# Attention and a two-layer MLP in one pass: the first score blocks and the due times of batches 1 to 3

## The chip, the cores and the metric

The kernel runs on one core of a Trainium2 chip. The metric is device time in microseconds (us) of one execution. Before the change three runs took 661.99, 661.43 and 659.28 us; their median is 661.43 us.

## The reference

Causal attention over 4 batches, 12 heads, 448 positions and 64 dimensions, all in fp32, feeds an MLP whose middle is h · clip(h + 3, 0, 6) / 6:

```python
scores = scale * np.matmul(q, k.transpose(0, 1, 3, 2))
scores = np.where(np.triu(ones, k=1), -1e9, scores)
attn = np.exp(scores - max(scores)); attn = attn / (sum(attn) + 1e-09)
x = np.matmul(attn, v)            # to 1792 tokens x 768
h = x @ w_in                      # 768 x 2048
g = h * np.clip(h + 3.0, 0.0, 6.0) / 6.0
return (g @ w_out).astype(np.float32)   # 2048 x 768
```

## The kernel before

**Tiles.** The 448 positions are cut in four blocks of 112 (C). Two heads make a pair; there are six pairs (NPAIR) of each batch. The first block of all four batches at once is done by `first_pair` (six times, pairs 0 to 5), since it only attends to itself: scores 112x112 for each batch and head, with the four batches side by side in a tile of 112x448. The other three blocks of a batch are done by `pair`, 24 times. The MLP runs in five groups: group 0 on the 448 tokens of the first blocks, groups 1 to 4 on the 336 other tokens of batches 0 to 3. A group is 96 steps: 16 blocks of 128 rows of `w_in` (three steps each) and six of 128 outputs of `w_out` (eight steps each).

**Precision.** Each fp32 factor is split into a high part and a remainder (`xh`, `xl` of the input, `wh`, `wl` of a weight, `gh`, `gl` of the gate), and `triple` makes three matmuls of each product: lines 598 to 600. In group 0 the weights come as pairs of 32-bit words of int64 and the values are put together by three bit operations on VectorE for each chunk of 384 or 512 columns (`bits`, lines 571, 573 and 576) before the cast to `wh` (ScalarE) and the subtraction for `wl` (GpSimd or VectorE); the result is also kept in DRAM for the groups behind. A block of `w_in` has two chunks, so six bit operations.

**first_pair before.** On TensorE: the mask is added by a matmul (line 322), then 16 instructions of products q·k (329). On VectorE: row maximum of either head (336). The two heads then go different ways. Head 1: the maximum is scaled (342), and ScalarE makes four exponentials of 112x112 (348), each with its own bias and a sum given out by an extra accumulator read. Head 0: VectorE subtracts the maximum (356), ScalarE makes one exponential of 112x448 (360), VectorE sums (363). Then for both heads the inverse of the sums (369, 370), the scaling on GpSimd (377), a transpose on TensorE into bank `mo` (386), a copy to `pt` on ScalarE or VectorE (238 or 241), the product with v (399), and `x_split` into `xh` and `xl`. A matmul of group 0 reads the `x` of all six pairs, so group 0 starts when pair 5 is through.

**What sets the order.** The class `Flow` plans everything ahead: each operation has a key (a due time in steps), the engines that may do it with an assumed duration, and the buffers it needs; at each moment an engine of the plan takes the ready operation of lowest key. What the planner decides is then written out as a fixed order of each engine; on the chip every engine works through its own list in order. The assumed durations thus set the order and nothing else. All DMAs are issued by SyncE (SP), in the planned order. Keys of the first loads are near -900; `T_FIRST`, `T_EARLY` and `T_REST` are the due times of the first blocks, of the pairs of batch 0 (every 13 steps), and of the pairs of batches 1 to 3 (every 16 steps).

PSUM has eight banks: six `s` (scores, bit operations, transposes and products with v of `pair`) and two `mo` (accumulators of the MLP, transposes of `first_pair`). There are three buffers each of `wh`, `wl` and `op` (weight words put together, and operands of `pair`) and four of `wd` (raw weight words).

Of the kernel before, what the change touches and what calls it, by code (L numbers as in the profile page):

```python
# [50 lines left out]
T_FIRST, T_EARLY, T_REST, T_LOAD, T_W, T_WLOAD = -66, 4, -16, -24, 9, 9  # L51
# [139 lines left out]
def tile_causal_attention_hardswish_moe(ctx: ExitStack, tc: tile.TileContext, q, k, v, w_in, w_out, out):  # L191
# [66 lines left out]
    three = const.tile([128, 1], F32, tag="three", name="three")  # L258

    def setup():  # L260
# [12 lines left out]
        nc.vector.tensor_copy(maskr, mask[:, R:].unsqueeze(1).to_broadcast([C, B, C]))  # L273
# [20 lines left out]
    def by_batch(x):  # L294
        return x.rearrange("m (b s) -> m b s", b=B)

    def first_pair(p):
        t = T_FIRST + 8 * p
        for a, src in enumerate((q, k)):
            dma(  # L300
                -900 + 4 * p, 230e3, lambda a=a: by_batch(ap(first_qk)[:, 2 * p + a]),
                lambda src=src: src[:, p, :, :, :C].rearrange("b e d s -> (e d) b s"),
                w=[(first_qk, p, a)],
            )
# [29 lines left out]
        for e in (1, 0):  # L334
            one(
                t + 1, {"D": 1}, elem(S), lambda _, e=e: nc.vector.tensor_reduce(row(e, 0), sc[e](), AX.X, ALU.max),
                [(ps[e], 0)], [(st, e, 0)],
            )
            if e:
                one(  # L340
                    t + 1, {"D": 1}, .25,
                    lambda _: nc.vector.tensor_scalar(row(1, 0), row(1, 0), -0.125, None, ALU.mult),
                    [], [(st, 1, 0)],
                )
        for b in range(B):
            one(
                t + 2, {"A": 1}, .6,
                lambda _, b=b: nc.scalar.activation(
                    pb[1]()[:, b], sc[1]()[:, b], ACTF.Exp, bias=ap(st)[:, 1, b:b + 1], scale=0.125,
                    accum_out=ap(st)[:, 1, 4 + b:5 + b],  # L350
                ),
                [(ps[1], 0), (st, 1, 0)], [(pr[1], b), (st, 1, 4 + b)],
            )
        allb = [(pr[0], b) for b in range(B)]
        one(
            t + 2, {"D": 1}, elem(S), lambda _: nc.vector.tensor_tensor(pb[0](), sc[0](), wide(0, 0), ALU.subtract),
            [(ps[0], 0), (st, 0, 0)], allb,
        )
        one(
            t + 2, {"A": 1}, .65, lambda _: nc.scalar.activation(pb[0](), pb[0](), ACTF.Exp, scale=0.125), [], allb,  # L360
        )
        one(
            t + 3, {"D": 1}, elem(S), lambda _: nc.vector.tensor_reduce(row(0, 4), pb[0](), AX.X, ALU.add),
            allb, [(st, 0, 4)],
        )
# [6 lines left out]
        sums = [(st, 0, 4)] + [(st, 1, 4 + b) for b in range(B)]  # L372
        one(t + 3.5, {"D": 1}, .5, inverse, [], sums + [("sums", p)])
        for e in (1, 0):
# [5 lines left out]
                sums, [(pr[e], b) for b in range(B)],  # L380
# [7 lines left out]
            pe(t + 10 - e, [(.4, turn, [(tp, 0)])], [(pr[e], b) for b in range(B)])  # L388
# [213 lines left out]
    def group(g):  # L602
# [107 lines left out]
```

## Time and profile before

| what | value |
|---|---|
| median of three runs | 661.43 us (659.28 to 661.99) |
| the profiled execution | 661.54 us |
| its span, first to last instruction | 659.8 us |
| TensorE busy | 643.9 us, 98% |
| VectorE / ScalarE / GpSimd busy | 71% / 56% / 46% |
| mean granted TensorE clock | 0.992 of 2.4 GHz |

The profiled execution is 1.7 us longer than its span, which is the time around the first and the last instruction. A busy TensorE is not a TensorE at its peak: matmuls overlap, and a matmul counts as busy from its start to its modelled end. Where the spacing of matmuls matters, the starts of rows are compared. A line of the timeline has the start, the duration from that start to the end of the last of its instructions, the engine, the line of code, the tiles, a count and, in brackets, the idle time before it and what ended that.

### The profile page before, as it was taken

To read this page: it belongs to the slowest core of one execution; us is meant where nothing else is said; L and a number is where in the kernel's file an instruction comes from. 1 tells how busy PE (TensorE), PEld (TensorE's weight loads), DVE (VectorE), ACT (ScalarE), POOL (GpSimd) and SP (SyncE) were. 2 spreads that over 40 slices of the span, in tenths; PEclk is the share of its full clock that TensorE was granted. 3 is DMA by queue.
4 is the path that set the end of the run, shared out by engine and by line. 5 is a ranking of instruction groups with operands and counts; after the bars stand their busy time and mean duration, and the time that the engine had idled before them with its cause. 6 is when DMAs were issued, how large, how long until landed. Compare 5 with 4: busy or idle time off the path is not lost.

```text
span 659.8 us, 12245 instructions
## 1 busy us (share of the span) xinstructions
PE 643.9 (98%) x4236; PEld 587.3 (89%) x4236; DVE 465.8 (71%) x939; ACT 367.3 (56%) x870; POOL 301.2 (46%) x333
## 2 busy tenths in 40 slices
PE   7689999999999999999999999999999999999998
PEld 5569887878889999999999999999999999999997
DVE  4889898977687798854588795567798743566432
ACT  3665656654546666555576664656666554444342
POOL 1667667546572686423375563433676410011100
PEclk9979999999999999999999999999999999999999
DMA  9989876888788543556744547555553334643452
GB/s 232 259 267 298 265 242 192 260 282 295 206 265 246 158 144 107 159 171 182 217 152 135 154 127 206 157 168 186 161 168 87 112 113 132 209 139 110 139 164 65
DMA packets 66878, 120.89 MB, mean 183 GB/s; under 512 B 16896, under 2 KB 33408, under 8 KB 66816
## 3 DMA queue, kind: packets, MB, share of 16 engines
q1 hardware_dynamic: 66816, 120.11, 60.7%
q8 instruction: 33, 0.54, 0.3%
q14 instruction: 29, 0.24, 0.1%
HBM read 101.99 MB, written 18.09 MB: 182 GB/s over the span
## 4 chain that ended last, share of the span: by engine, by line
PE 92%; DVE 3%; DMA 1%; SPq 1%; ACT 1%; POOL 1%; issue 1%; DVEq 0%; ACTq 0%; POOLq 0%
PE mo L598 24%; PE mo L600 23%; PE mo L599 23%; PE s L535 6%; PE s L516 6%; PE s L450 3%; PE s L451 2%; PE s L453 2%; DMA gh<-in_k_dram 1%; SPq L229 1%; PE s L399 1%; DVE s L571 1%; DVE s L573 1%; DVE op L576 0%; PE s L329 0%
## 5 line engine op out<-in xcount | busy, mean ns | idle before, releaser
L250 DVE TENSOR_TENSOR wl<-wd,wh 128x512 fp32r<-128x512 f32 (+1 forms) x159 | 142.8, 898 | 99.8 <-ACT wh L238 99.5
L238 ACT CAST wh<-wd 128x512 fp32r<-128x512 f32 (+1 forms) x160 | 112.9, 706 | 120.0 <-PE mo L599 85.9
L598 PE MATMUL mo<-xh,wh 128*128 128x336 f32 (+1 forms) x480 | 160.8, 335 | 0.1
L598 PE MATMUL mo<-gh,wh 128*128 128x336 f32 (+1 forms) x480 | 159.2, 332 | 0.0
L600 PE MATMUL mo<-xh,wl 128*128 128x336 f32 (+1 forms) x480 | 157.2, 327 | 0.0
L600 PE MATMUL mo<-gh,wl 128*128 128x336 f32 (+1 forms) x480 | 156.9, 327 | 0.3 <-POOL wl L250 0.3
L599 PE MATMUL mo<-gl,wh 128*128 128x336 f32 (+1 forms) x480 | 156.4, 326 | 0.0
L599 PE MATMUL mo<-xl,wh 128*128 128x336 f32 (+1 forms) x480 | 156.2, 325 | 0.0
L505 POOL TENSOR_SCALAR pr<-pr,prow 112x224 f32<-112x224 f32 x144 | 109.0, 773 | 39.5 <-DVE prow L493 39.3
L476 DVE CUSTOM_DVE_ANT_0 s<-s,mask 112x448 f32<-112x448 f32 (+1 forms) x144 | 70.6, 527 | 39.7 <-PE s L451 33.1
L245 POOL TENSOR_SCALAR gh<-r 128x336 fp32r<-128x336 f32 x51 | 33.3, 654 | 138.2 <-DVE r L627 128.6
L598 PEld LDWEIGHTS mo<-xh,wh 128*128 128x128 f32 x480 | 91.0, 190 | 5.8 <-issue 1.7
L598 PEld LDWEIGHTS mo<-gh,wh 128*128 128x128 f32 x480 | 90.3, 188 | 2.8 <-issue 0.8
L599 PEld LDWEIGHTS mo<-xl,wh 128*128 128x128 f32 x480 | 91.4, 190 | 1.1
L600 PEld LDWEIGHTS mo<-gh,wl 128*128 128x128 f32 x480 | 90.2, 188 | 2.2 <-POOL wl L250 0.6
L600 PEld LDWEIGHTS mo<-xh,wl 128*128 128x128 f32 x480 | 90.6, 189 | 1.3
L599 PEld LDWEIGHTS mo<-gl,wh 128*128 128x128 f32 x480 | 90.3, 188 | 1.3
L483 ACT ACTIVATE pr<-s,prow 112x448 f32<-112x448 f32 (+1 forms) x144 | 76.9, 542 | 25.7 <-DVE prow L476 25.7
L250 POOL TENSOR_TENSOR wl<-op,wh 128x512 fp32r<-128x512 f32 (+1 forms) x35 | 53.3, 1522 | 44.1 <-ACT wh L238 34.3
L238 ACT COPY pt<-s 112x336 f32<-112x336 f32 x139 | 53.3, 446 | 26.0 <-PE s L516 25.9
L621 ACT ACTIVATE r<-mo,three 128x336 f32<-128x336 f32 (+1 forms) x80 | 44.7, 558 | 26.4 <-PE mo L600 20.9
L245 POOL TENSOR_SCALAR op<-qk 128x784 fp32r<-128x784 f32 x31 | 30.4, 985 | 57.3 <-PE s L451 54.0
(70 smaller groups left out, 853.6 us busy)
## 6 DMA issues: line engine op xcount, KB each, us to landing
wd<-kept_w SPq DMA_DIRECT2D x64, 384.0 KB, 3.3
wd<-kept_w SPq DMA_DIRECT2D x96, 256.0 KB, 2.7
wd<-in_w_in_dram SPq DMA_DIRECT2D x16, 768.0 KB, 5.7
wd<-in_w_out_dram SPq DMA_DIRECT2D x24, 512.0 KB, 5.2
qk<-in_k_dram SPq DMA_DIRECT2D x84, 112.0 KB, 2.7
qk<-in_q_dram SPq DMA_DIRECT2D x84, 84.0 KB, 2.6
kept_w<-op SPq DMA_DIRECT2D x16, 384.0 KB, 5.7
kept_w<-op SPq DMA_DIRECT2D x24, 256.0 KB, 5.4
```

The lines of the kernel that those rows point to most:

```text
L238: nc.scalar.copy(o(), i()) if scale is None else nc.scalar.mul(o(), i(), scale)
L245: nc.gpsimd.tensor_scalar(o(), i(), 1.0, 1.0, ALU.mult, ALU.mult)
L250: (nc.gpsimd if e == "P" else nc.vector).tensor_tensor(o(), a(), b(), ALU.subtract)
L476: lambda _, e=e, i=i, w=w, dst=dst: nc.vector.tensor_tensor_reduce(dst(), dst(), mask[:, S - w:], -0.125, 3.0e38, ALU.add, ALU.min, ap(st) ...
L483: lambda _, e=e, i=i, dst=dst: nc.scalar.activation(ap(pr[e, i]), dst(), ACTF.Exp, bias=ap(st)[:, e, i:i + 1], scale=-1.0, accum_out=ap(st ...
L505: nc.gpsimd.tensor_scalar(x, x, r, 1.0, ALU.mult, ALU.mult)
L516: nc.tensor.transpose(ap(tp)[:C, C * o:C * o + C], ap(pr[e, i])[:, C * j:C * j + C], ident)
L535: nc.tensor.matmul(ap(av)[64 * e:64 * e + 64, R - w:R], ap(vr)[:, j, e, :], ap(ph)[:, o:o + w], start=(j == 0), stop=(j == NC_ - 1),)
L598: nc.tensor.matmul(ps, ap(wh)[:, a], xh, start=start, stop=False)
L599: nc.tensor.matmul(ps, ap(wh)[:, a], xl, start=False, stop=False)
L600: nc.tensor.matmul(ps, ap(wl)[:, a], xh, start=False, stop=stop)
L621: lambda _, r=r, acc=acc: nc.scalar.activation(ap(r)[:, :n], ap(acc)[:, :n], ACTF.Relu, bias=three, scale=1.0),
```

## The change

Four things change. (1) The loads of the first blocks: q and k of a pair are issued earlier against v and against the first four weight blocks, whose loads now stand behind nearly all of q, k and v. (2) In `first_pair` head 1 is done as head 0: subtraction on VectorE, one exponential on ScalarE, sum on VectorE; the scaled maximum and the four exponentials with accumulator reads are gone. The planner's assumed durations for these are other numbers. (3) A small exponential on a constant at the start brings the load of ScalarE's function table ahead. (4) `T_REST` is -10 and was -16: every operation of batches 1 to 3, its loads included, has a due time six steps later.

```diff
-T_FIRST, T_EARLY, T_REST, T_LOAD, T_W, T_WLOAD = -66, 4, -16, -24, 9, 9
+T_FIRST, T_EARLY, T_REST, T_LOAD, T_W, T_WLOAD = -66, 4, -10, -24, 9, 9
...
+        nc.scalar.activation(warm, three, ACTF.Exp)
...
-                -900 + 4 * p, 230e3, lambda a=a: by_batch(ap(first_qk)[:, 2 * p + a]),
+                -900 + 4 * p - 6, 230e3, lambda a=a: by_batch(ap(first_qk)[:, 2 * p + a]),
...
-        for e in (1, 0):
+        for e in range(2):
+            allb = [(pr[e], 0)]
             one(
-                t + 1, {"D": 1}, elem(S), lambda _, e=e: nc.vector.tensor_reduce(row(e, 0), sc[e](), AX.X, ALU.max),
+                t + 1, {"D": 1}, .61, lambda _, e=e: nc.vector.tensor_reduce(row(e, 0), sc[e](), AX.X, ALU.max),
...
-            if e:
-                one(
-                    t + 1, {"D": 1}, .25,
-                    lambda _: nc.vector.tensor_scalar(row(1, 0), row(1, 0), -0.125, None, ALU.mult),
...
-        for b in range(B):
             one(
-                t + 2, {"A": 1}, .6,
-                lambda _, b=b: nc.scalar.activation(
-                    pb[1]()[:, b], sc[1]()[:, b], ACTF.Exp, bias=ap(st)[:, 1, b:b + 1], scale=0.125,
-                    accum_out=ap(st)[:, 1, 4 + b:5 + b],
...
+                t + 2, {"D": 1}, .62,
+                lambda _, e=e: nc.vector.tensor_tensor(pb[e](), sc[e](), wide(e, 0), ALU.subtract),
...
+                t + 2, {"A": 1}, .6, lambda _, e=e: nc.scalar.activation(pb[e](), pb[e](), ACTF.Exp, scale=0.125),
...
+                t + 3, {"D": 1}, .61, lambda _, e=e: nc.vector.tensor_reduce(row(e, 4), pb[e](), AX.X, ALU.add),
...
-            wh, wl = weights(g, i, t, -900 + 4 * i + 11 if not g and i < 4 else None)
+            wh, wl = weights(g, i, t, -900 + (17 if not i else 21 + 4 * i) if not g and i < 4 else None)
```

Since the planner orders everything anew, the lists of the engines differ nearly from the first row. Three places show what moved. In the changed file the lines of `first_pair` and of what follows stand up to 11 lower (maximum 339, subtraction 344, exponential 348, sum 352, inverse 358 and 359, transpose 375, product with v 388, bit operations 560, 562 and 565).

SyncE's list at the start (`gh` takes q and k, `gl` takes v, `wd` raw weights; a row of 128x4x112 or 112x4x128 is 224 KB, one of 128x1536 768 KB). Before, from the seventh load on, that is pair 2 and pair 3 with the first weight block between them:

```order
L229 DMA gh<-in_q_dram 128x4x112
L229 DMA gh<-in_k_dram 128x4x112
L229 DMA gl<-in_v_dram 112x4x128
L229 DMA wd<-in_w_in_dram 128x1536
L229 DMA gh<-in_q_dram 128x4x112
L229 DMA gh<-in_k_dram 128x4x112
L229 DMA gl<-in_v_dram 112x4x128
```

Now, from the twelfth load on, that is q and k of pair 4:

```order
L229 DMA gh<-in_q_dram 128x4x112
L229 DMA gh<-in_k_dram 128x4x112
L229 DMA gl<-in_v_dram 112x4x128
L229 DMA gh<-in_q_dram 128x4x112
L229 DMA gh<-in_k_dram 128x4x112
L229 DMA gl<-in_v_dram 112x4x128
L229 DMA wd<-in_w_in_dram 128x1536
L229 DMA gl<-in_v_dram 112x4x128
L229 DMA wd<-in_w_in_dram 128x1536 x3
```

The k of pairs 0 to 5 is load 2, 5, 8, 12, 16 and 20 before, with one, two and three weight loads ahead of the last three; now it is load 2, 4, 7, 10, 13 and 16 with no weight load ahead of any.

TensorE's list behind the products of pairs 0 and 1 (`s<-gh` products, eight for a pair; `mo<-ident` transposes; `s<-pt,gl` product with v). Before:

```order
L322 MATMUL s<-maskr,identr 112x448 x2
L329 MATMUL s<-gh 112x112 x8
L322 MATMUL s<-maskr,identr 112x448 x2
L386 MATMUL mo<-ident,pr_215 112x112 x4
L386 MATMUL mo<-ident,pr_225 112x112 x4
L329 MATMUL s<-gh 112x112 x8
L399 MATMUL s<-pt_289,gl 64x112
```

Now:

```order
L324 MATMUL s<-maskr,identr 112x448 x2
L331 MATMUL s<-gh 112x112 x16
L375 MATMUL mo<-ident,pr_226 112x112 x4
L324 MATMUL s<-maskr,identr 112x448 x2
L375 MATMUL mo<-ident,pr_224 112x112 x4
L331 MATMUL s<-gh 112x112 x8
L388 MATMUL s<-pt_285,gl 64x112
```

Pairs 2 and 3 (x16) now stand ahead of pair 0's transposes, and pair 4's products (x8) ahead of pair 0's product with v; behind that product (eight rows) come pair 1's transposes, whose copies to `pt` VectorE makes.

VectorE's list around the inverse of the sums of pair 5 (`L336` and `L363` reductions, `L369` and `L370` inverse, `L571`, `L573`, `L576` bit operations, ISA with `mask` the masked maximum of `pair`). Before, where both chunks of the first weight block have been done far earlier:

```order
L363 TENSOR_REDUCE prow<-pr_422 112x4
L369 TENSOR_SCALAR prow<-prow 112x2x4
L370 RECIPROCAL prow<-prow 112x2x4
L356 TENSOR_TENSOR pr_468<-s,prow 112x448
L476 ISA s,prow<-s,mask 112x448
L476 ISA prow 112x1
L363 TENSOR_REDUCE prow<-pr_468 112x4
L369 TENSOR_SCALAR prow<-prow 112x2x4
L370 RECIPROCAL prow<-prow 112x2x4
L571 TENSOR_SCALAR s<-wd 128x384
L573 SCALAR_TENSOR_TENSOR s<-wd,s 128x384
L576 SCALAR_TENSOR_TENSOR op<-wd,s 128x384
```

Now, with the first chunk of the first weight block in it:

```order
L344 TENSOR_TENSOR pr_454<-s,prow 112x448
L344 TENSOR_TENSOR pr_458<-s,prow 112x448
L560 TENSOR_SCALAR s<-wd 128x384
L562 SCALAR_TENSOR_TENSOR s<-wd,s 128x384
L565 SCALAR_TENSOR_TENSOR op<-wd,s 128x384
L352 TENSOR_REDUCE prow<-pr_454 112x4
L352 TENSOR_REDUCE prow<-pr_458 112x4
L358 TENSOR_SCALAR prow<-prow 112x2x4
L359 RECIPROCAL prow<-prow 112x2x4
L465 ISA s,prow<-s,mask 112x448
L465 ISA prow 112x1
L465 ISA s,prow<-s,mask 112x448
```

Behind these rows stand two more masked maxima (112x336) and then the second chunk of the first weight block. The three bit operations behind pair 5's inverse are those of the second weight block before and, after the four masked maxima, of the first weight block now. The first matmul of group 0 has 126 matmuls of the program ahead of it on TensorE in either kernel, the same ones in another order.

## Rows read from the trace of the kernel before

**Rows 1.** The page: TensorE's busy time, and its granted clock in 40 slices.

```profile
PE 643.9 (98%) x4236; PEld 587.3 (89%) x4236; DVE 465.8 (71%) x939; ACT 367.3 (56%) x870; POOL 301.2 (46%) x333
PEclk9979999999999999999999999999999999999999
```

**Rows 2.** Busy time by stretch; columns: stretch, length, then each engine, clock, DMA.

```profile
6.70:45.00 38.30, 28.71 (x242) 21.30 (x242) 30.61 (x69) 24.98 (x82) 19.47 (x18) 0.91 0.97 251
45.00:56.00 11.00, 10.87 (x50) 9.57 (x47) 10.47 (x26) 6.07 (x14) 6.45 (x6) 0.84 1.04 368
```

**Rows 3.** Waits of TensorE, whole span: us in total, times, longest.

```profile
PE s L399 <- ACT pr L483: 1.8, 1, 1.8
PE mo L600 <- POOL wl L250: 0.3, 1, 0.3
```

**Rows 4.** Timeline of TensorE, 4 to 46 us.

```profile
4.89 1.84 PE L329 MATMUL s<-gh 64*112 64x112 f32 x16
8.85 1.84 PE L329 MATMUL s<-gh 64*112 64x112 f32 x16 [2.12 <-DMA gh<-in_k_dram]
12.01 1.84 PE L329 MATMUL s<-gh 64*112 64x112 f32 x16 [0.30 <-DMA gh<-in_k_dram]
17.23 1.84 PE L329 MATMUL s<-gh 64*112 64x112 f32 x16 [0.49 <-DMA gh<-in_k_dram]
19.00 1.76 PE L399 MATMUL s<-pt,gl 112*64 112x112 f32 x16
20.69 1.60 PE L386 MATMUL mo<-ident,pr 112*112 112x112 f32 x8
28.39 1.04 PE L329 MATMUL s<-gh 64*112 64x112 f32 x16
45.20 0.48 PE L598 MATMUL mo<-xh,wh 128*128 128x448 f32 x1
45.71 0.39 PE L600 MATMUL mo<-xh,wl 128*128 128x448 f32 x1
```

**Rows 5.** Loads of `gh` issued at 17.4 us: issue, and time to landing.

```profile
L229 SPq DMA_DIRECT2D gh<-in_k_dram x1: 2467/2467/2467, 17.4 to 17.4; - x1
...
DMA to landing us min/median/max: 10.1/10.1/10.1
```

**Rows 6.** VectorE by line, 0 to 45 us: busy us, mean ns, idle before.

```profile
L336 DVE TENSOR_REDUCE prow<-s 112x4 f32<-112x448 f32 x12 | 7.4, 614 | 6.6 <-PE s L329 6.6
L356 DVE TENSOR_TENSOR pr<-s,prow 112x448 f32<-112x448 f32 x6 | 3.7, 624 | 1.4 <-PE mo L386 1.1
L363 DVE TENSOR_REDUCE prow<-pr 112x4 f32<-112x448 f32 x6 | 3.6, 608 | 0.0
L342 DVE TENSOR_SCALAR prow<-prow 112x4 f32<-112x4 f32 x6 | 1.2, 201 | 0.2
```

**Rows 7.** Timeline of VectorE, operations that follow each other without a wait.

```profile
31.69 0.61 DVE L336 TENSOR_REDUCE prow<-s 112x4 f32<-112x448 f32 x1
32.22 0.60 DVE L363 TENSOR_REDUCE prow<-pr 112x4 f32<-112x448 f32 x1
32.86 0.17 DVE L369 TENSOR_SCALAR prow<-prow 112x8 f32<-112x8 f32 x1
37.01 0.54 DVE L571 TENSOR_SCALAR s<-wd 128x384 int32<-128x384 int32 x1
37.58 0.56 DVE L573 SCALAR_TENSOR_TENSOR s<-wd,s 128x384 int32<-128x384 int32 x1
```

**Rows 8.** Timeline, ScalarE and GpSimd: cast and remainder of a weight block.

```profile
46.16 0.85 ACT L238 CAST wh<-op 128x768 fp32r<-128x768 f32 x1
47.46 1.83 POOL L250 TENSOR_TENSOR wl<-op,wh 128x768 fp32r<-128x768 f32 x1
```

**Rows 9.** Waits of VectorE, 45 to 118 us.

```profile
DVE r L627 <- ACT r L621: 3.5, 6, 1.1
```

More of the change, by code (lines that the diff above doesn't have):

```diff
@@ L258, in tile_causal_attention_hardswish_moe @@
     three = const.tile([128, 1], F32, tag="three", name="three")
+    warm = const.tile([128, 1], F32, tag="warm", name="warm")
     def setup():
@@ L333, in first_pair @@
         pe(t, [(1.1, products, keys)], [(first_qk, p, 0), (first_qk, p, 1)], True)
-        for e in (1, 0):
+        for e in range(2):
+            allb = [(pr[e], 0)]
             one(
-                t + 1, {"D": 1}, elem(S), lambda _, e=e: nc.vector.tensor_reduce(row(e, 0), sc[e](), AX.X, ALU.max),
+                t + 1, {"D": 1}, .61, lambda _, e=e: nc.vector.tensor_reduce(row(e, 0), sc[e](), AX.X, ALU.max),
                 [(ps[e], 0)], [(st, e, 0)],
             )
-            if e:
-                one(
-                    t + 1, {"D": 1}, .25,
-                    lambda _: nc.vector.tensor_scalar(row(1, 0), row(1, 0), -0.125, None, ALU.mult),
-                    [], [(st, 1, 0)],
-                )
-        for b in range(B):
-            one(
-                t + 2, {"A": 1}, .6,
-                lambda _, b=b: nc.scalar.activation(
-                    pb[1]()[:, b], sc[1]()[:, b], ACTF.Exp, bias=ap(st)[:, 1, b:b + 1], scale=0.125,
-                    accum_out=ap(st)[:, 1, 4 + b:5 + b],
-                ),
-                [(ps[1], 0), (st, 1, 0)], [(pr[1], b), (st, 1, 4 + b)],
-            )
[L354 to L365, printed above, removed]
+            one(
+                t + 2, {"D": 1}, .62,
+                lambda _, e=e: nc.vector.tensor_tensor(pb[e](), sc[e](), wide(e, 0), ALU.subtract),
+                [(ps[e], 0), (st, e, 0)], allb,
+            )
+            one(
+                t + 2, {"A": 1}, .6, lambda _, e=e: nc.scalar.activation(pb[e](), pb[e](), ACTF.Exp, scale=0.125),
+                [], allb,
+            )
+            one(
+                t + 3, {"D": 1}, .61, lambda _, e=e: nc.vector.tensor_reduce(row(e, 4), pb[e](), AX.X, ALU.add),
+                allb, [(st, e, 4)],
+            )
         def inverse(_):
@@ L370, in inverse @@
             nc.vector.reciprocal(r, r)
-        sums = [(st, 0, 4)] + [(st, 1, 4 + b) for b in range(B)]
+        sums = [(st, e, 4) for e in range(2)]
         one(t + 3.5, {"D": 1}, .5, inverse, [], sums + [("sums", p)])
@@ L379, in first_pair @@
                 ),
-                sums, [(pr[e], b) for b in range(B)],
+                sums, [(pr[e], 0)],
             )
@@ L386, in turn @@
                     nc.tensor.transpose(ap(tp)[:C, C * b:C * b + C], pb[e]()[:, b], ident)
-            pe(t + 10 - e, [(.4, turn, [(tp, 0)])], [(pr[e], b) for b in range(B)])
+            pe(t + 10 - e, [(.4, turn, [(tp, 0)])], [(pr[e], 0)])
             move(
```

## The prediction

> **What bounds the kernel now.** First the page: TensorE is busy for 643.9 of 659.8 us, so what is not TensorE's own work is at most some 16 us [rows 1]. Then its waits over the whole span: behind the start of group 0 only one is left, 0.3 us on a late `wl`; the longest of the others shown is 1.8 us ahead of the last product with v [rows 3]. The work of TensorE is the same before and after, so the time can change in two ways: group 0 starts at another moment, or TensorE has to wait behind it. Group 0 starts at 45.20, its first use of a `wl` at 45.71 [rows 4]. The timeline up to there is read for what holds that moment. Products of pairs 1, 2 and 3 wait for their k (8.85, 12.01, 17.23); pair 5's start at 28.39, and the load of its k, issued at 17.4, took 10.1 us, so it landed at 27.5 [rows 4, 5]. So the loads bound the first 28 us, and a chain through VectorE, GpSimd, TensorE and ScalarE takes the other 17. VectorE is busy for 30.6 of 38.3 us between 6.7 and 45, and 6.6 us of its idle time are waits of the row maximum for products [rows 2, 6]: 7.7 us is all that earlier loads can win from it. The clock row has a 7 in its third slice (33 to 49 us) [rows 1], and 45 to 56 us has 0.84 [rows 2].
>
> **The loads.** A 224 KB load costs what lies between the products that wait for them: from 4.89 to 8.85 three loads, 1.32 us each; from 8.85 to 12.01 three, 1.05 each; from 12.01 to 17.23 three and a 768 KB one, so 5.22 − 3 × 1.18 = 1.7 us for that [rows 4]. In the new order the k of pair 4 is load 13, eleven behind pair 0's: 4.9 + 11 × 1.18 = 17.9 us (16.4 to 19.4 by the two ends). The k of pair 5 is load 16: 4.9 + 14 × 1.18 = 21.4, six us ahead of 27.5. The first weight block is load 18 and lands near 24.3; its bit operations come to VectorE near 35 by the walk below, so putting it off costs nothing; were VectorE ten us quicker than I reckon, it would.
>
> **VectorE.** Each pair loses one operation of 0.20 and gets a subtraction of 0.62 and a sum of 0.61, so six pairs bring 6 × 1.03 = 6.2 us more busy time [rows 6]. That is nearly the 7.7 us that the loads can free. The Trainium skill ("VectorE: DVE Perf Modes", its table of rules near the end) calls `tensor_reduce` the slowest VectorE operation and advises to restructure it away, which speaks against the new sums. Here the sum takes 608 ns and the subtraction 624 [rows 6], so the trace does not bear that out; the sum below has both at one price.
>
> Now the path. New on TensorE is that pair 4's products stand ahead of pair 0's product with v, and that ahead of pair 1's transposes. Behind the k at 17.9 come these products (17.23 to 19.00, so 1.77), the product with v (19.00 to 20.69, 1.69) and four of the eight transposes in 1.60 (0.8) [rows 4]: VectorE's first copy of pair 1 can start at 22.2. VectorE would reach it by some 18, after the maxima, subtractions and sums of two pairs and a half; so it waits for about 4 us, and is dense behind it. From that copy to the second chunk of the first weight block the list has 23 operations of 448 columns (copies, maxima, subtractions, sums), eight small ones, six bit operations and four masked maxima. Operations of 448 columns follow each other by 0.53 (31.69 to 32.22), a small one on a sum by 0.64, that is 0.1 more, and 0.2 behind it; bit operations by 0.57 [rows 7]. So 23 × 0.54 + 4 × (0.1 + 0.2 + 0.2) + 6 × 0.58 + 4 × 0.5 = 12.4 + 2.0 + 3.5 + 2.0 = 19.9, and the first weight block is put together at 42.1. The cast takes 0.85 and the remainder on GpSimd 1.83 [rows 8], with two hand-overs of 0.2 the first `wl` is there at 45.2. Pair 5 is ready by then: its inverse ends 2.0 + 1.75 = 3.8 us before 42.1, near 38.3; scaling, transposes, copies and the product with v took 8 us from inverse to group 0's start before (37.1 to 45.2, the operation at 37.01 follows that inverse [rows 4, 7]), which is 46.3 by that measure. But before, part of it was the 1.8 us wait for a copy that stood behind an exponential [rows 3]; without it 44.5. So group 0 starts near 43.5 to 44.5 and its first `wl` matmul near 45.3, against 45.71: **−0.4 us**. Bounds: with k at 16.4 and TensorE at its full rate already (products in 1.04 as at 28.39 [rows 4]) 3.4 us earlier (1.5 and 1.9); with k at 19.4 and the exponential again in the way 1.9 later.
>
> **ScalarE.** 24 exponentials and as many accumulator reads turn into six; the table load moves to where the engine is idle. Nothing on the path above waits for an exponential, so this is put at 0. If the path ran over ScalarE instead, it would be a gain within the bounds given.
>
> **The clock.** After group 0's start its matmuls are not 0.2 us apart: 45 to 56 us has 0.84 of the full clock [rows 2], that is 11 × 0.16 = 1.8 us given away at the lower of the two levels. It follows upon the 1.8 us wait [rows 3]. In the new order TensorE waits for the first `wl` for a like time, so I take the loss as it was: 0; bounds −1.8 and +0.5.
>
> **VectorE behind the start.** At 45.2 it had put together two weight blocks and half of a third before; now, by the walk above, it is five bit operations into the second. That is some 4 operations, less one masked maximum done more: 1.8 us behind. Its waits from 45 to 118 us are 3.5 us, all on the gate for ScalarE's result of a block that TensorE has just finished [rows 9]; these are waits of an engine that is ahead, and they pay for it. 0; if they stay where they are, up to +1.8.
>
> **Batches 1 to 3 six steps later.** Their matmuls, loads, casts (GpSimd) and subtractions all move by six steps, some 5.5 us. Group 0's last blocks get `op` buffers and VectorE to themselves for longer, where the 0.3 us wait for a `wl` is [rows 3]: −0.3. The last pair of a batch is through some 14 us ahead of the first matmul that reads it (about 90 matmuls stand between in the new list, about 150 in the old), and `x_split` needs two to three us: 0. There is no more to win, as TensorE does not wait there; bounds −0.3 and +1.
>
> **The sum.** Against the profiled execution, 661.54 us (span 659.8 and 1.7 around it, 0.1 above the median): −0.4 + 0 + 0 − 0.3 = −0.7, so **660.8 us**, no change that a measurement could tell. Such a one needs 0.5%, 3.3 us.
>
> **Rivals.** *Faster: the loads count in full.* If TensorE is at its higher level from the first blocks on, pair 4's products and the product with v take 1.0 each, the copies start at 20.3 and all behind it 1.9 earlier; with k at the early end 3.4 us; without the low stretch behind 45 another 1.8. VectorE, then late, gives back up to 1.5: 661.5 − 3.4 − 1.8 − 0.3 + 1.5 = 657.5. For it: the products take 1.84 us up to 17.23 and 1.04 at 28.39, so the rate is there to be had [rows 4]. Against: VectorE has no 5 us to give. *Slower: VectorE's list becomes the bound of group 0.* The two further operations of a pair and the first weight block now stand in one queue; if pair 5's inverse ends later than 40.5 us, the start slips by 1.9, and when TensorE then catches up with `wl` after `wl` in blocks 4 to 15 the 1.8 us come on top: 661.5 + 1.9 + 1.8 − 0.3 = 664.9; a contended copy or two more make 666. For it: VectorE is busy for 10.5 of 11 us behind the start [rows 2]. Against: its 3.5 us of waits. *Same, by the pairs:* the later batches press on the group changes and cost 1: 661.8.
>
> **How the numbers follow.** My forecast with the pairs' case 0.64, faster 0.18, slower 0.18. The range takes the forecast's own bounds and most of both others: 657.2 to 665.2. Faster by over 0.5% means under 658.2, slower over 664.8: 0.17 and 0.17, within 0.66.
>
> **What would show it.** Products of pairs 4 and 5 start near 18 and under 25 us. VectorE waits for TensorE ahead of a copy to `pt` between 18 and 22, then hardly until 42. The inverse of pair 5 ends near 38, the first matmul of group 0 starts near 44, its first `wl` matmul waits until 45.3. No wait of TensorE over 1 us behind 60 us. The forecast is wrong if that copy starts by 19, if group 0 starts before 42 or after 47, or if waits for `wl` add up to over 2 us.

## The result: slower by 0.6%, and where the time stands in the profile after

| | before | after |
|---|---|---|
| median | 660.94 us | 664.58 us |
| ratio after to before, 95% interval | | 1.0059, 1.0040 to 1.0079 |
| profiled execution, its span | 661.54, 659.8 us | 663.56, 661.5 us |

The forecast was 660.8, a change of -0.7; measured is +3.6. The profiled execution of the changed kernel is the fastest of its six, that of before is near the slowest of its own, so the two traces stand only 2.0 us apart (1.7 of them in the span) and can account for no more than that.

The page of the changed kernel first, busy time and clock, to be held against [rows 1]:

```profile
PE 641.7 (97%) x4236; PEld 583.3 (88%) x4236; DVE 472.2 (71%) x949; ACT 357.2 (54%) x816; POOL 311.5 (47%) x342
PEclk9899999999999999999999999999999999999999
```

The 7 of the third slice is gone; an 8 stands in the second. The timeline of TensorE in the changed kernel, as [rows 4] (products of a pair are now L331, its product with v L388, the MLP L587 to L589):

```profile
4.86 1.84 PE L331 MATMUL s<-gh 64*112 64x112 f32 x16
7.59 1.84 PE L331 MATMUL s<-gh 64*112 64x112 f32 x16 [0.89 <-DMA gh<-in_k_dram]
10.40 1.84 PE L331 MATMUL s<-gh 64*112 64x112 f32 x16
13.25 1.04 PE L331 MATMUL s<-gh 64*112 64x112 f32 x16 [1.00 <-DMA gh<-in_k_dram]
16.11 1.04 PE L331 MATMUL s<-gh 64*112 64x112 f32 x16 [0.51 <-DMA gh<-in_k_dram]
19.53 1.04 PE L331 MATMUL s<-gh 64*112 64x112 f32 x16
40.30 0.47 PE L587 MATMUL mo<-xh,wh 128*128 128x448 f32 x1
42.07 0.47 PE L589 MATMUL mo<-xh,wl 128*128 128x448 f32 x1 [1.10 <-POOL wl L250]
50.41 0.47 PE L587 MATMUL mo<-xh,wh 128*128 128x448 f32 x1 [1.27 <-DVE r L616]
```

Group 0 starts at 40.30, not 45.20, and its first matmul with a `wl` at 42.07, not 45.71: 3.6 us earlier. So the loss lies behind the start. The waits of TensorE from 56 us to the end (the three largest; us in total, times, longest), where before has one of 0.3 for a `wl` and one of 0.4 ahead of a transpose, which [rows 3] does not show:

```profile
PE s L505 <- POOL pr L494: 1.6, 4, 0.6
PE s L505 <- ACT pt L238: 0.9, 2, 0.6
PE mo L587 <- DVE r L616: 0.6, 2, 0.4
```

To place it, the starts of the same MLP matmul are compared (TensorE does the 2880 MLP matmuls in one sequence in every kernel here, 576 for a group). A mark g:n is matmul n of group g, both counted from 0: 0:2 is the first with a `wl`, 4:0 the first of group 4. Minus is earlier than in the profile of before. Each row is one execution, and the last column says how far that execution is from the median of its kernel's runs; the one of before is 0.6 over its own. So an end that is one or two us off says little by itself: the 7.6 of e1 is 4.3 by the medians, and the -1.7 of e13 is +1.4. Marks in groups 1 to 3 of a kernel with a later due time look early, as fewer operations of pairs stand ahead of them; the first of group 4 has all pairs behind it in any kernel.

| kernel (profiled execution) | 0:0 | 0:2 | 0:96 | 0:384 | 4:0 | end | this execution to its median |
|---|---|---|---|---|---|---|---|
| changed | -4.9 | -3.6 | -2.5 | -2.4 | +1.7 | +1.7 | -1.0 |
| new first blocks, old due time (e1) | -3.5 | -2.3 | -1.3 | -1.2 | +7.5 | +7.6 | +4.1 |
| old first blocks, later due time (e2) | -0.8 | -0.4 | -0.8 | -0.8 | +3.5 | +3.5 | +0.3 |
| loads alone (e3) | +6.0 | +6.4 | +7.5 | +4.5 | +10.6 | +10.6 | +2.4 |
| exponentials alone (e4) | -3.1 | -1.9 | -0.8 | -0.6 | +4.2 | +4.2 | +0.2 |
| new first blocks, old order of the rest (e9) | -3.6 | -3.6 | +6.2 | +6.2 | +6.1 | +6.1 | -1.0 |
| old first blocks, changed order of the rest (e10) | -1.1 | -0.6 | +0.1 | +0.2 | +4.3 | +4.3 | +1.0 |
| new first blocks, old order from step 45 (e12) | -2.7 | -1.4 | -0.3 | -0.3 | -0.4 | -0.4 | +0.7 |
| new first blocks, old order from step 0 (e14) | -2.6 | -2.2 | -1.9 | -1.7 | -1.9 | -1.9 | -1.2 |
| changed, remainders on VectorE (e13) | -5.6 | -4.4 | -3.2 | -3.1 | -1.7 | -1.7 | -2.0 |

In the changed kernel 3.6 us are won up to the first `wl`, 1.1 given back on balance over the next blocks (waits of 1.27 and 0.37 for gates), and **4.2 us lost between 0:96 and 4:0**, where my forecast had -0.3.

### The profile page after: what moved, and what is told of

It reads as the page before. It is cut to its first block, busy times and chain, and to the rows that moved or that the text cites. A ratio compares the mean times of both kernels' runs of the same rounds, so it can differ in the third digit from the quotient of the medians.

```text
span 661.5 us, 12187 instructions
## 1 busy us (share of the span) xinstructions
PE 641.7 (97%) x4236; PEld 583.3 (88%) x4236; DVE 472.2 (71%) x949; ACT 357.2 (54%) x816; POOL 311.5 (47%) x342
## 4 chain that ended last, share of the span: by engine, by line
PE 60%; DVE 2%; POOL 2%; ACT 0%; issue 0%; DMA 0%; SPq 0%; DVEq 0%; ACTq 0%
PE mo L587 16%; PE mo L589 16%; PE mo L588 15%; PE s L524 5%; PE s L505 4%; PE s L439 2%; PE s L440 2%; POOL pr L494 2%; DVE gl L250 1%; DVE r L616 0%; DVE op L250 0%; DMA qk<-in_k_dram 0%; POOL gh L245 0%; DVE kl L250 0%; ACT pr L472 0%
## 5 line engine op out<-in xcount | busy, mean ns | idle before, releaser
L250 DVE TENSOR_TENSOR wl<-wd,wh 128x512 fp32r<-128x512 f32 (+1 forms) x147 | 130.8, 891 | 104.1 <-ACT wh L238 101.6
L587 PE MATMUL mo<-xh,wh 128*128 128x336 f32 (+1 forms) x480 | 161.4, 336 | 2.3 <-DVE r L616 2.3
L587 PE MATMUL mo<-gh,wh 128*128 128x336 f32 (+1 forms) x480 | 159.4, 332 | 0.0
L589 PE MATMUL mo<-xh,wl 128*128 128x336 f32 (+1 forms) x480 | 156.2, 325 | 1.1 <-POOL wl L250 1.1
L589 PE MATMUL mo<-gh,wl 128*128 128x336 f32 (+1 forms) x480 | 156.9, 327 | 0.0
L587 PEld LDWEIGHTS mo<-xh,wh 128*128 128x128 f32 x480 | 90.3, 188 | 8.7 <-DVE r L616 3.8
L587 PEld LDWEIGHTS mo<-gh,wh 128*128 128x128 f32 x480 | 90.3, 188 | 3.9 <-issue 1.2
L589 PEld LDWEIGHTS mo<-xh,wl 128*128 128x128 f32 x480 | 90.3, 188 | 3.1 <-POOL wl L250 1.5
L589 PEld LDWEIGHTS mo<-gh,wl 128*128 128x128 f32 x480 | 90.2, 188 | 1.8 <-POOL wl L250 0.2
L245 POOL TENSOR_SCALAR gh<-r 128x336 fp32r<-128x336 f32 x48 | 27.0, 563 | 108.9 <-DVE r L616 101.5
L250 POOL TENSOR_TENSOR wl<-op,wh 128x512 fp32r<-128x512 f32 (+1 forms) x37 | 56.1, 1518 | 46.9 <-ACT wh L238 38.5
L238 ACT COPY pt<-s 112x336 f32<-112x336 f32 x132 | 51.1, 445 | 28.2 <-PE s L505 28.1
L505 PE MATMUL s<-ident,pr 112*112 112x112 f32 x432 | 52.7, 260 | 2.6 <-POOL pr L494 1.6
```

The costliest lines, as they stand in the source:

```text
L238: nc.scalar.copy(o(), i()) if scale is None else nc.scalar.mul(o(), i(), scale)
L245: nc.gpsimd.tensor_scalar(o(), i(), 1.0, 1.0, ALU.mult, ALU.mult)
L250: (nc.gpsimd if e == "P" else nc.vector).tensor_tensor(o(), a(), b(), ALU.subtract)
L505: nc.tensor.transpose(ap(tp)[:C, C * o:C * o + C], ap(pr[e, i])[:, C * j:C * j + C], ident)
L587: nc.tensor.matmul(ps, ap(wh)[:, a], xh, start=start, stop=False)
L589: nc.tensor.matmul(ps, ap(wl)[:, a], xh, start=False, stop=stop)
```

## The experiments

**By parts.** First the due time against the rest of the change, and the change of the first blocks in its two halves.

```diff
 e1: changed kernel with  T_REST = -16        e2: kernel before with  T_REST = -10
 e3: kernel before with
-                -900 + 4 * p, 230e3, lambda a=a: by_batch(ap(first_qk)[:, 2 * p + a]),
+                -900 + 4 * p - 6, 230e3, lambda a=a: by_batch(ap(first_qk)[:, 2 * p + a]),
-            wh, wl = weights(g, i, t, -900 + 4 * i + 11 if not g and i < 4 else None)
+            wh, wl = weights(g, i, t, -900 + (17 if not i else 21 + 4 * i) if not g and i < 4 else None)
 e4: e1 with these two lines as before
```

> The changed kernel with the due time of batches 1 to 3 put back (T_REST = -16), so only the first blocks are changed: loads, exponentials, warm-up. In the trace of the changed kernel group 0's first matmul with a wl stands 3.6 us earlier than before (42.07 against 45.71) and the matmuls 1.5 to 2.5 us earlier up to the start of group 2; behind that it loses 4 us up to the end of group 3. Theory 1 (the due time costs the 4 us): this kernel keeps the gain of the head, 2.3 to 2.5 us, and ends near 658.5 (ratio 0.996); TensorE's gaps behind 200 us are those of the kernel before. Theory 2 (any new plan of groups 1 to 3 costs this much, because the planner places the pairs anew once the head is changed): it loses the 4 us as well, 662 to 664. Theory 3 (the new first blocks themselves cost time): 661 or more with group 0 starting late or waiting in blocks 4 to 15.

> The kernel before with T_REST = -10 and nothing else. Theory 1 (the due time costs about 4 us in groups 1 to 3): 664.5 to 665 (ratio 1.006), the head as before with the first matmul of group 0 near 45, and the loss again behind 200 us, as transposes of the pairs that wait for GpSimd's scaling. Theory 2 (a matter of a new plan, of either sign): anything between 659 and 663, with no loss where the pairs of batches 2 and 3 run. By my forecast's own term for this edit it would be 660.6 (-0.3).

> The kernel before with the new keys of the first loads only (q and k of a pair earlier, the first four weight blocks behind them). Theory 1a (the loads carry the head's gain): the products of pair 5 start under 22 us and group 0 starts 3 us earlier or more; ratio 0.996 to 0.998, some 1.5 to 2.5 us faster. Theory 1b (the loads free time that four small exponentials and their accumulator reads then take back on ScalarE): group 0 starts within 1 us of 45.2, ratio 0.999 to 1.001.

> The kernel before with the new exponentials (both heads by subtraction, one exponential and a sum) and the small early exponential, with the old loads and the old due time. Theory 1a (the loads bound the first 28 us): pair 5's products still start near 28 us, group 0 starts near 45, VectorE's 6.2 us more go into its waits; ratio 0.999 to 1.002. Theory 1b (ScalarE's chain of exponentials was what held the later pairs): group 0 starts 2 us earlier or more, ratio 0.996 to 0.998.

Measured, before 660.70 beside them:

| | T_REST = -16 | T_REST = -10 |
|---|---|---|
| first blocks as before | 660.70 | 664.75 (1.0059, 1.0045 to 1.0073) |
| first blocks changed | 664.96 (1.0074, 1.0052 to 1.0095) | 664.58 (1.0059, 1.0040 to 1.0079) |

The loads alone give 669.99 (1.0124, 1.0099 to 1.0150), the exponentials alone 665.57 (1.0070, 1.0056 to 1.0084). Theory 1, that the due time alone costs the 4 us, falls: either half of the change costs about 4 us alone, and both together no more. So does the thought that the loads make the earlier start: with the exponentials alone group 0 starts 3.1 us earlier though pair 5's products still start at 27.31, and with the loads alone 6.0 us later. The two rows of e4:

```profile
27.31 1.04 PE L331 MATMUL s<-gh 64*112 64x112 f32 x16
42.05 0.48 PE L587 MATMUL mo<-xh,wh 128*128 128x448 f32 x1
```

In e3 pair 5's products start 6 us earlier than before, but its last product with v is through near 46.3, one us later than before. The other 4.9 us up to group 0's start are products of one more pair of batch 0, which this plan puts ahead of it:

```profile
22.33 1.04 PE L329 MATMUL s<-gh 64*112 64x112 f32 x16
46.25 1.01 PE L453 MATMUL s<-qk 64*112 64x448 f32 x4
51.17 0.74 PE L598 MATMUL mo<-xh,wh 128*128 128x448 f32 x1
```

Where e1 loses, in an execution 4.1 us over the median of its runs: first its waits of TensorE from 180 to 240 us (total, times, longest), of which before has only the 0.3 us of [rows 3].

```profile
PE s L439 <- DVE op L250: 1.8, 2, 1.4
PE mo L587 <- DVE r L616: 1.2, 1, 1.2
PE mo L589 <- DVE wl L250: 1.0, 1, 1.0
```

Then, among the waits of VectorE in e1 from 160 to 215 us, the longest:

```profile
DVE op L565 <- DMA kept_w<-op: 7.8, 4, 4.5
```

And the stretch from 200 to 210 us in e1, columns as [rows 2]:

```profile
200.00:210.00 10.00, 7.43 (x27) 6.41 (x26) 8.39 (x17) 3.38 (x9) 7.07 (x10) 0.66 0.74 216
```

VectorE cannot write the next weight words, as all three `op` buffers are held, by stores of earlier words to DRAM. The same wait is 2.4 us before, 5.8, 9.1 and 6.8 in the other three, and 0.3 in the changed kernel, which loses its time elsewhere. TensorE then waits at the change from group 0 to group 1, and behind these waits its granted clock falls: 0.66 in the mean of that stretch, with matmuls of 448 columns at 0.57 us for a time, the level of 1.2 GHz, in place of 0.37. Before, the same stretch has 1.00 and TensorE busy for 10.00 us:

```profile
200.00:210.00 10.00, 10.00 (x64) 8.53 (x63) 7.42 (x15) 5.08 (x11) 0.99 (x2) 1.00 0.84 253
```

**A fourth `op` buffer, and a due time half way.**

```diff
 e5: e1, e6: kernel before, e7: changed kernel, each with
-    gh=1, gl=1, prow=3, r=4, qk=4, op=3, kl=3, vr=3, wh=3, wl=3, pr3=4, pr2=3, pr1=3,
+    gh=1, gl=1, prow=3, r=4, qk=4, op=4, kl=3, vr=3, wh=3, wl=3, pr3=4, pr2=3, pr1=3,
 e8: changed kernel with  T_REST = -13
```

> The new first blocks with the old due time (T_REST = -16), and a fourth op buffer. With three, VectorE waited 7.8 us between 160 and 215 us (four times, up to 4.5) for stores of weight words to DRAM to free an op buffer, and TensorE waited 4.3 us at the change from group 0 to group 1 and fell to 0.66 of its clock for 10 us. Theory O (op buffers held by stores make the stall of the group change): with a fourth buffer that wait goes below 2 us, TensorE waits under 1 us between 180 and 240, and the kernel keeps the head's gain: 657 to 660 (ratio 0.995 to 0.998). Theory P (every order planned anew loses 4 us somewhere, whatever is relieved): 663 to 666 with the stall moved to another place.

> Control: the kernel before with a fourth op buffer alone. Theory O: VectorE's 2.4 us of waits for stores go, TensorE had no wait left there, so nothing is gained: 660 to 661.5 (ratio 0.998 to 1.001). Theory P: a new order, so 663 to 666 like the four others that changed the order.

> The changed kernel with a fourth op buffer (due time -10). It has no stall at the group change but some 5 us of short TensorE waits between 200 and 570 us, ahead of transposes whose scaling on GpSimd came late. Theory O: these are not for op buffers, so it stays at 663 to 665.5 (ratio 1.003 to 1.007). If op buffers hold the pairs' operands back too (their split goes through op), 659 to 661.

> The changed kernel with T_REST = -13, half way. If the due time trades the stall at the group change (with -16) against late pairs in groups 1 to 3 (with -10) smoothly, half of each: 660 to 664, with TensorE waits of 1 to 2 us at 190 to 210 and gaps of 2 to 3 us behind 220. If the order is what counts and not the due time, anything between 658 and 668, and the waits in a place that neither neighbour shows.

e5 662.15 (1.0014, 0.9999 to 1.0028), e6 663.08 (1.0031, 1.0017 to 1.0045), e7 662.23 (1.0010, 0.9996 to 1.0025), e8 667.50 (1.0096, 1.0072 to 1.0119), before 660.50. With the fourth buffer TensorE has no wait left between 180 and 240 us in e5 and VectorE none for a store, and e5 is 2.8 us shorter than e1. That fits a stall made by the held buffers; as e5's order is new as well, it does not prove it. The kernel before loses 2.6 by the same buffer, and -13 is worse than -10 and -16: the sign does not follow from what an edit relieves. What all these kernels but the one before have in common is that the planner ordered everything anew.

**Holding the order.** The planner is run twice. The second run may start the operations of pairs and groups only in the order, and on the engines, of the first, and a buffer only behind those that first blocks took ahead of it there.

```diff
+        if self.follow:
+            for e in lists:
+                mine = [self.ops[self.heads + n] for x, n in self.follow if x == e]
+                mine = [o for o in mine if o.key[0] >= T_HELD]
+                for i, o in enumerate(mine):
+                    rank[o] = i
+                    o.ways = {e: (o.ways[e][0], 0)}
...
+                    if o in rank and (turn[e] != rank[o] or any(
+                        not b.held and not before[b.tag, b.number] <= done[b.tag] for b in o.bufs
+                    )):
+                        continue
...
+    _, follow, taken = describe(first_pair_before, lambda i: -900 + 4 * i + 11)
+    order, _, _ = describe(first_pair, lambda i: -900 + (17 if not i else 21 + 4 * i), follow, taken)
```

e9 holds all that is not `first_pair`; e10 has the two lines at the end the other way round, with `T_REST = -10`; e11 is e9 with four `op` buffers on the chip. e12 and e14 hold only what is due from step 45 and from step 0 on (`T_HELD`).

> The new first blocks (loads, exponentials, warm-up), with everything behind first_pair held to the order and the engines that the kernel before has: the planner is run on the kernel before, and the second run may start the operations of the pairs and groups on each engine in that order only. TensorE's list of pairs and groups is the same, row for row; the same holds for the bit operations, casts, remainders and loads. Theory A (the new first blocks gain some 2.5 us and the re-ordered rest loses more): group 0's first matmul with a wl stands 2.5 to 3.5 us earlier, the distance to before hardly changes behind 215 us, and the time is 657.5 to 659.5 (ratio 0.995 to 0.998). Theory B (the rest has a bound of its own, such as VectorE's weight words or the stores of them, and takes an earlier start back whatever the order): 660 to 661.5, with TensorE waiting for weights before 205 us. Theory C (the new first blocks harm): over 662.

> The cross: the first blocks of the kernel before, with everything behind them held to the order of the changed kernel (planned with T_REST = -10 behind the new first blocks). Theory A: the order of the rest carries the loss, 4.5 to 6.5 us against before: 665 to 667.5 (ratio 1.007 to 1.010), TensorE waiting for late scalings near 224 and 267 us as in the changed kernel. Theory B: 662 to 664. Theory C: near 661, as the harm is gone with the new first blocks.

> As the kernel with the new first blocks and the old order of the rest, but with a fourth op buffer on the chip, while the order is still that which the planner made with three. A fourth op buffer alone cost 2.6 us before, which by theory A is the new order that came with it and not the buffer: here, with the order held, it costs nothing and frees VectorE from waits for stores (2.4 us before, 160 to 215): 0 to 1 us less than the same kernel with three, 657 to 659. If the buffer itself costs (by where the tiles then lie in memory), 1 to 3 us more.

> The new first blocks and the old due time, group 0's first half as the planner now makes it, and from due step 45 on (second half of group 0 and all behind it) the order and engines of the kernel before. The kernel held from the first blocks on lost 10 us in 45 to 60 us, because VectorE waited 6 us for a PSUM bank that pair 5 still had, and nothing behind. Theory A (order of the rest carries the loss; the old order takes any start without loss): the loss of 3 to 8 us at the change of groups that the same first blocks have with a free plan goes, the difference to before stays within 0.5 us behind 215 us, and the time is before less what the first blocks win by 100 us, 1 to 2.5 us: 658.5 to 660. Theory B (weight words, stores and loads of group 0 bound its end, whatever the order): the gain is used up by 215 us as waits for weights or op buffers, 660.5 to 662.

> As the kernel held from step 45, but the old order from due step 0 on, with the operations due before group 0's first step free (the bit operations of the first weight blocks among them). The free plan and the changed kernel lose 2 us more than before between 56 and 120 us, as transposes of batch 0's pairs wait for bit operations and copies. Theory A: with the old order these go, and the gain is that of the start: 3 to 3.5 us, 657 to 658.5. Against it: the start may again meet a bank that is held, as in the kernel held from the first blocks, then 662 or more with a VectorE wait of some us between 40 and 60.

e9 668.60 (1.0127, 1.0101 to 1.0153), where I had expected 658.5; e11 668.65 (1.0122, 1.0109 to 1.0135), so that the fourth buffer by itself, with the order held, makes no difference that can be seen there (a small gain could hide behind e9's late start, told next); e10 664.87 (1.0059, 1.0046 to 1.0073). What went wrong in e9 stands in one row of VectorE's timeline (its lines are up to 130 higher):

```profile
42.70 0.56 DVE L701 TENSOR_SCALAR s<-wd 128x384 int32<-128x384 int32 x1 [6.00 <-ACT r L268]
```

And what follows from it in one of TensorE's, of e9 too:

```profile
59.09 0.74 PE L728 MATMUL mo<-xh,wh 128*128 128x448 f32 x1 [5.08 <-DVE r L757]
```

In the held order the second weight block's bit operations take their PSUM bank behind pair 5's product with v; VectorE, which now has nothing else, stands still for 6.0 us, is behind with the weights, and the gate comes 5.1 us late. But from 0:48 (+6.3) to the end (+6.1) nothing more is lost. And e10, with the first blocks of before, loses between 0:96 and 4:0 what the changed kernel loses there: 4.2 us in both, and 4.3 by its median. So the 4.2 us belong to the order of the rest and not to what stands ahead of it.

With the first rows left free, e12 gives 660.36 (0.9993, 0.9981 to 1.0004) and e14 660.79 (0.9997, 0.9984 to 1.0010), before 660.45: against e1, the same edits in a free plan, 4.6 and 4.2 us less. From 0:96 on their distance to before stays within 0.2 us. So the old order takes the loss away; but neither is faster than before, where I had expected 658.5 to 660 and 657 to 658.5. The lead of 1.9 us in e14's trace is nearly all its own execution, 1.2 under its median, and that of before, 0.6 over: that the earlier start is worth any time is not shown. The waits of TensorE from 60 us to the end in e12 are two kinds:

```profile
PE s L648 <- ACT pt L270: 0.9, 2, 0.6
PE s L648 <- DVE op L708: 0.2, 1, 0.2
```

From 200 to 300 us TensorE is busy throughout in e12 (columns as [rows 2]), where the changed kernel, the second row, has 98.39:

```profile
200.00:300.00 100.00, 100.00 (x687) 93.58 (x686) 76.67 (x155) 61.33 (x146) 52.54 (x59) 1.00 0.54 161
200.00:300.00 100.00, 98.39 (x677) 90.77 (x676) 78.72 (x163) 59.40 (x147) 56.50 (x63) 1.00 0.51 149
```

**What in the changed order costs.** First VectorE's timeline from 211 to 222 us in the changed kernel.

```profile
211.51 2.97 DVE L250 TENSOR_TENSOR gl<-r,gh 128x336 fp32r<-128x336 f32 x1
...
215.91 1.44 DVE L250 TENSOR_TENSOR gl<-r,gh 128x336 fp32r<-128x336 f32 x1
217.28 1.33 DVE L250 TENSOR_TENSOR kl<-qk,op 128x448 fp32r<-128x448 f32 x1
...
220.77 0.51 DVE L250 TENSOR_TENSOR gl<-r,gh 128x336 fp32r<-128x336 f32 x1 [0.67 <-POOL gh L245]
221.20 0.16 DVE L481 TENSOR_SCALAR prow<-prow 112x6 f32<-112x6 f32 x1
221.40 0.19 DVE L482 RECIPROCAL prow<-prow 112x6 f32<-112x6 f32 x1
```

Then GpSimd's of the same stretch:

```profile
211.44 1.87 POOL L250 TENSOR_TENSOR wl<-wd,wh 128x768 fp32r<-128x768 f32 x1
213.28 0.85 POOL L245 TENSOR_SCALAR op<-qk 128x784 fp32r<-128x784 f32 x1
...
215.84 1.15 POOL L250 TENSOR_TENSOR kl<-qk,op 128x448 fp32r<-128x448 f32 x1
217.07 1.06 POOL L250 TENSOR_TENSOR op<-qk,op 64x336 fp32r<-64x336 f32 x1
...
221.76 5.49 POOL L494 TENSOR_SCALAR pr<-pr,prow 112x224 f32<-112x224 f32 x6 [1.02 <-ACT xh L238]
```

And the transposes on TensorE that wait for one of these scalings:

```profile
225.03 0.69 PE L505 MATMUL s<-ident,pr 112*112 112x112 f32 x5 [0.55 <-POOL pr L494]
```

The subtraction that makes `gl` takes 0.51 us where GpSimd is idle and 1.44 to 2.97 us where it subtracts too; in the row of 2.97 a copy of GpSimd's follows its subtraction. The Trainium skill ("SBUF — State Buffer", section "Who interferes with whom") says that a VectorE instruction with two inputs in SBUF contends with a GpSimd instruction that reads SBUF; the trace agrees, by 2.97 against 0.51 us. The rows of 2.97, 1.44 and 1.33 end 0.35, 0.36 and 0.48 us behind the end of a GpSimd row (214.13, 216.99, 218.13): it looks as if VectorE stood until GpSimd was through, and not as if both went on slowly. The inverse (221.40) stands behind these on VectorE, the six scalings behind the inverse on GpSimd, and a transpose waits. The row of the scalings names a cast on ScalarE, but they start 0.17 us behind the inverse's end (221.59), and as much behind it in the kernel of the next experiment, where another cast is named (220.04 behind 219.87). GpSimd is idle for 1.02 us ahead of them in both, so at this place its own list does not hold them up. Before, one remainder of groups 1 to 4 is on GpSimd; in the changed order 13 are. In e13 these 13 are issued to VectorE, in an order that is otherwise the changed kernel's.

```diff
-            emit(e)
+            emit("D" if e == "P" and emit in rest_wl else e)
```

> The changed kernel in its own order, but the 13 remainders of weight blocks of groups 1 to 4 that its plan gives to GpSimd are issued to VectorE at the same place. Theory G (while GpSimd subtracts, VectorE's subtractions take 1.3 to 1.5 us in place of 0.5 to 0.7, so inverse and scaling of a pair come late and transposes on TensorE wait): the waits ahead of transposes at 224 and 267 us shrink, lost time between 215 and 300 us falls from 10.8 towards 7 us, ratio to before 1.000 to 1.003. Rival V (VectorE's list itself is too long there): 13 more operations of 1.0 us on VectorE make these waits longer, ratio 1.006 to 1.012.

661.86 (1.0017, 1.0004 to 1.0031): 2.7 us less than the changed kernel, give or take some 1.6 (an estimate from the two intervals). Between 0:96 and 4:0 it loses 1.5, not 4.2, in an execution 2.0 us under its median. What each of the 13 is worth is not shown, nor whether at other pairs VectorE's shorter rows or GpSimd's shorter list won the time. From 200 to 300 us the 16 subtractions for `gl` take 746 ns in the mean and 964 in the changed kernel (786 before); of VectorE's groups of instructions by line there, first that of e13:

```profile
L250 DVE TENSOR_TENSOR gl<-r,gh 128x336 fp32r<-128x336 f32 x16 | 11.9, 746 | 2.2 <-POOL gh L245 2.2
```

The same group in the changed kernel:

```profile
L250 DVE TENSOR_TENSOR gl<-r,gh 128x336 fp32r<-128x336 f32 x16 | 15.4, 964 | 2.3 <-POOL gh L245 2.3
```

**Is that the due time's cost, and is there a better kernel?** The plans with -10 and -13 have 10 to 13 remainders on GpSimd, those with -16 one to five. e17 is e2 with its 11 on VectorE; e15 is e7 with its 10 there; e16 is e12 with a fourth buffer, held from step 60.

> The kernel before with T_REST = -10 (664.75, 4.05 over before), in that order, with the 11 remainders that it gives to GpSimd in groups 1 to 4 (1 in the kernel before) issued to VectorE. Theory G (the due time costs by moving remainders to GpSimd): the 3.1 us lost behind group 2's start go for the most part, 661.5 to 663 (ratio 1.002 to 1.004). Rival V (the late pairs themselves cost): 664 to 666.

> The changed kernel with a fourth op buffer, in the order the planner makes for that, and the 10 remainders that this order gives to GpSimd in groups 1 to 4 issued to VectorE. The fourth buffer took 2.4 us off the changed kernel (662.2), the remainders on VectorE 2.7 (661.9). If they act in different places, the two together give 659.5 to 660.5 (ratio 0.998 to 1.000); if the fourth buffer's order had already removed what the remainders cost, 661.5 to 662.5.

> New first blocks, fourth op buffer, free order up to due step 60 and from there the order of the kernel before. With the fourth buffer the free order was 3.3 to 5.0 us ahead of before 65 us after the start, without it 1.3 to 2.5, and the old order behind step 45 kept each start without loss. If that lead is real and kept, 657 to 659 (ratio 0.995 to 0.998). If the lead is only work of batch 0's pairs that stands later, 660 to 662.

e17 666.03 (1.0080, 1.0058 to 1.0103): not less than e2, so theory G does not hold there. Behind group 2's start it loses 2.0 where e2 loses 3.1, but between 0:384 and 2:0 it loses 3.8 where e2 loses 1.1: from 180 to 240 us TensorE waits for 3.0 us there and for 2.2 in e2, and from 190 to 200 us its clock is 0.83, not 1.00. The remainders on GpSimd cost 2.7 us in the changed order and, on balance, nothing in that of e2. e15 660.77 (1.0002, 0.9987 to 1.0016) and e16 660.59 (1.0006, 0.9993 to 1.0019) undo the loss but win nothing over before, 660.21. No kernel that was run beats the one before by more than its interval.

## Why the prediction was wrong, point by point

**The loads.** The k of pair 4 was there by 16.11 and that of pair 5 by 19.53, not 17.9 and 21.4. From 7.59 to 16.11 nine loads came, 0.95 us each; I had 1.18, and the early bound, 16.4, was the right one.

**TensorE in the first blocks.** I took 1.77, 1.69 and 0.8 us for what stands behind pair 4's k. But the products of pair 3 take 1.04 at 13.25 already, the higher of the two levels: from 7.59 on TensorE has products and masks with waits of no more than 1.0 us between them, where before one of 2.1 stood ahead of pair 1's [rows 4]. That this made the difference is not shown: in e4 the products of pair 1 take 1.04 behind a wait of 1.7. VectorE was through with its work ahead of the first copy of pair 1 at 17.7, as forecast, but the copy starts at 18.64, not 22.2. I had written that a copy by 19, or group 0's start before 42, would prove the forecast wrong; both came. Three rows of VectorE in the changed kernel, the copy, the end of pair 5's inverse and the first block's last bit operation:

```profile
18.64 1.16 DVE L241 COPY pt<-mo 112x448 f32<-112x448 f32 x2 [0.90 <-PE mo L375]
34.13 0.20 DVE L359 RECIPROCAL prow<-prow 112x8 f32<-112x8 f32 x1
38.69 0.55 DVE L565 SCALAR_TENSOR_TENSOR op<-wd,s 128x384 int32<-128x384 int32 x1
```

**VectorE's walk** was right in size: from 18.64 to the second chunk of the first block at 39.24 (the row of 38.69 plus 0.55) are 20.6 us against 19.9, a wait of 1.1 included. With the copy 3.6 us earlier, the inverse of pair 5 ends at 34.3 (38.3 forecast) and the first `wl` matmul stands 3.6 earlier, not 0.4. My bound of 3.4 had this case, and the rival "the loads count in full" its two causes.

**ScalarE at 0** was wrong. The exponentials alone bring the start 3.1 us forward, the loads alone put it off by 6.0. In e4 pair 5's products start 1.1 us earlier than before (27.31) and the chain from there to the start takes 14.7 us, not 16.8 [rows 4]: the old start was bounded by that chain as much as by the load. As e4 has a new order too, that ScalarE alone won this is not shown. The rows of the forecast left out the chain's longest wait, 2.4 us of TensorE for a scaling on GpSimd:

```profile
PE mo L386 <- POOL pr L377: 2.7, 2, 2.4
```

**The clock, and VectorE behind the start.** I took both at 0. From 45 to 56 us the clock is 1.00, not 0.84 [rows 2], so the 1.8 us were there to win, and 18 matmuls on (0:18) the lead is 5.1 us; but VectorE is behind by then and TensorE waits 1.6 us for gates, so by 0:96 the lead has shrunk to 2.5. Here is the line of the changed kernel that answers to [rows 2]:

```profile
45.00:56.00 11.00, 9.36 (x46) 8.06 (x45) 10.48 (x24) 5.89 (x12) 6.35 (x5) 1.00 1.03 362
```

**"Batches 1 to 3 six steps later", -0.3, is the step that failed.** The edit alone costs 4.05 us (e2), and the changed kernel loses 4.2 between 0:96 and 4:0; the bounds were -0.3 and +1. I priced a due time: the operations slide by six steps, and `x_split` has slack. But a due time is an input of a planner that orders all engines again. The loss, as far as it was traced, is not where the step moves something but in what the new lists put side by side: 13 remainders on GpSimd against one, worth 2.7 of the 4.2 in the changed kernel. The other 1.5 are not traced to a row; and as e17 won nothing by moving its 11, why the edit alone costs 4.05 with the old first blocks stays open. "TensorE does not wait there, so there is no more to win" was true, and was the warning: a stretch without waits can only lose by a new order. Putting the due time back is no cure, as e1 shows: with -16 the new first blocks lose at the change of groups instead.

**The rivals.** "VectorE's list becomes the bound of group 0" gave 664.9 and so by luck the measured time, but not the mechanism: pair 5's inverse came at 34.3, not later than 40.5, and the start was earlier. The right account takes the first rival's start and four times the loss that the pairs' case put on the later batches. Left open is why all nine plans that the planner made freely for an edited kernel (the changed one and e1 to e8) have medians 1.6 to 9.3 us over before (for e5 and e7, the least of these, the interval of the ratio includes 1). For e1 the held `op` buffers fit; that the old order was a lucky one is likely by their number, but not shown.

## What to carry to other kernels

Where a planner or scheduler writes the order, an edit has two prices: what it does at its place, and what the new order does to everything else. Measure the first with the order of the rest held, before judging the edit by its time. Where the kernel before has no waits of its bound engine, expect the second to be a loss (none of nine new plans was faster here), and look in the new lists for what changed engine, not only for what changed place.

## What the runs showed of the hardware

A VectorE subtraction of two SBUF tiles took up to 2.97 us instead of 0.51 while GpSimd did a subtraction and a copy of its own, and ended 0.35 us behind them; over the span both engines were far from busy (71% and 47%), and it reached TensorE only through an inverse on VectorE and six scalings on GpSimd. In this kernel VectorE may write an `op` buffer again only when its store to DRAM has landed, 5.5 to 6.5 us after its issue in the page of the changed kernel; in e1 three buffers did not cover that, and VectorE waited up to 4.5 us at once:

```profile
kept_w<-op SPq DMA_DIRECT2D x16, 384.0 KB, 6.5
kept_w<-op SPq DMA_DIRECT2D x24, 256.0 KB, 5.5
```
